# Converting float64 weights in three rounds, and two early steps instead of three, in a Fourier filter and MLP kernel

## The chip, the cores and the metric

The kernel runs on one core of a Trainium2 chip. The metric is device time in microseconds (us); lower is better. A core has TensorE (PE; its weight loads are listed as PEld), VectorE (DVE), ScalarE (ACT), GpSimd (POOL) and the sequencer SP, which here only issues transfers. Transfers issued by SP, ScalarE and GpSimd are carried by DMA engines.

## The reference

```python
X = np.fft.rfft(x, axis=1)              # x: 8 x 3008 x 256
y = np.fft.irfft(X * (filt_r + 1j * filt_i), n=3008, axis=1)
x = y.reshape(24064, 256)
h = x @ w_in                            # 256 -> 2048
g = h - np.tanh(h)
out = g @ w_out                         # 2048 -> 256
```

x and the filters arrive as float32. The two weight matrices arrive as float64 and are computed with as float32, so the kernel itself has to convert them.

## The kernel before

**Transform.** 3008 is 64 times 47. A batch is transformed with matmuls in three stages with a round trip through DRAM between them. `first` (line 291) multiplies two slices of x by a 64-point matrix (`pf`, L304), copies the result on ScalarE (L305) and has ScalarE store it to `ct1`. `middle` (line 348) loads `ct1` as `a2`, makes the 47-point products (`pz`), multiplies them by the filter (`uv`, `zs`), transforms back (`pe`) and stores to `ct2`. `last` (line 436) loads `ct2` as `e2` (`load_e2`, L417 and L425), makes the inverse 64-point product (`pu`, L447) and copies it to `ut` on ScalarE (L449).

**MLP.** For every group of `ut` and every quarter of the 2048 columns there is one step, numbered U. `up` makes seven products by `wu` instead of eight (banks X, Y, Z, L483); between them ScalarE copies X out as s1, u2 and u3 (L489). `shrink` approximates h − tanh(h) with ScalarE activations (L539, 540, 545) and VectorE products (L544, 548), and ends with `combine` (L462 to 465), four GpSimd operations that make the combinations for the seven products of `down` by `wd` (L590). `down(U − 2)`, `shrink(U − 1)` and `up(U)` run interleaved. The order is written out by hand: `up` calls back d, e (a piece of `down`), s (a piece of `shrink`) and t(0) to t(4).

**Units.** The eight batches are worked in the units (0), (1, 2), (3, 4), (5, 6), (7). While one unit's MLP runs, the `first` and `middle` of the next are put between its products by t(k): a list of positions says from which t(k) on the next piece is due. The first pieces are the `first` steps of the next unit. For unit 0 there are 24 such steps, of which EARLY have been done before the loop; the rest are spread over the positions from 0.24 on, `1.36 * 24 / (24 - EARLY)` apart.

**Prologue.** Unit 0's transform has nothing to run beside it. It is written separately, as one hand-ordered block (from L861): x in three chunks, `first0` (its copies and stores), then a loop over j = 0 to 15. Step j makes `pz` (L915) for two frequencies, finishes the step before (`back0`: `pe` L896 and L898, copy e L901, store to `ct2` L902), and makes uv and zs on VectorE (L922, L923). One set of filters, c, serves two steps. `filters_of(c)` (L803) fetches it with six GpSimd transfers (L814), after two memsets (L822) for the first three sets; `double_filters` (L839, L840) and `turned` (L848, L849) complete it on ScalarE, in the odd step before its first use. The loads of a2, of the matrices `fg` and of x go out on SP.

**Weights.** `converted` (L191) turns one tile of 128 x 512 float64 words into float32. It loads the words (L197). VectorE takes the mantissa's upper bits (L204), the exponent (L207) and the sign (L210); ScalarE scales the mantissa (L205) and the exponent (L209); VectorE adds the lower word (L211). After a `yield` VectorE clamps the exponent (L214), shifts and joins it with the sign (L215) and multiplies into `wu` or `wd` (L222). `weights` (L225) is a generator that orders such jobs, two to a quarter of the columns of one matrix, and has GpSimd make four combinations of a finished quarter (`sums`, L255 to L258). The ten jobs of five quarters are drawn in the prologue, one `next(ws)` to each step j (three raw tiles, four tiles for the rest, the latter shared with the x chunks). The six jobs of the last three quarters are drawn from t(0), t(2) and t(4) of the main loop (`late`). There a job's tiles are borrowed from the transform's pool, two of each tag: raw from `ft`, `it` from `uv`, `pt` from `zs`, `st` from `e1`, `ft` from `a2`.

**Filter copies.** In t(1) and t(3) of the main loop `copies` draws from `filters_d`, which clears parts of DRAM from a tile `zero` (also of tag `a2`; L955, L962, L964) and copies the filters to DRAM with SP's transfers (L814).

**Handover.** In step j = 14 of the prologue `first(1)` starts, which asks for x 0 and 1 (`load_x`, L283, three tiles), followed by rows 0 to 48 of e2 (L417). After the last `back0` come rows 48 to 64 of e2, then EARLY steps of `first(1)`, each of which first asks for the x two steps on; then `last(0)` and the main loop.

Of the kernel before, what the change touches and what calls it, by code (L numbers as in the profile page):

```python
# [14 lines left out]
AF = mybir.ActivationFunctionType  # L15
ALU = mybir.AluOpType
# [7 lines left out]
NK = NQ // 2  # L24
# [6 lines left out]
IM = 64  # L31
# [7 lines left out]
UNITS = [(0,), (1, 2), (3, 4), (5, 6), (7,)]  # L39
HALF = (NR + 1) // 2  # L40

EARLY = 3


def steps_of(unit):
# [97 lines left out]
def kernel(  # L143
# [24 lines left out]
    def dram(t, off, dims):  # L168
        return bass.AP(tensor=t, offset=off, ap=[list(d) for d in dims])
# [21 lines left out]
    def converted(tiles, src, dsts, queue):  # L191

        n = src.shape[-1] * (src.shape[1] if len(src.shape) == 3 else 1)
        t = tiles("raw", I64, n)
        queue.dma_start(t if len(src.shape) == 2 else  # L197
                        t.rearrange("p (h n) -> p h n", h=src.shape[1]), src)
        yield
        words = t.bitcast(I32).rearrange("p (n w) -> p n w", w=2)  # L200
        lo, hi = words[:, :, 0].bitcast(U32), words[:, :, 1]
        it, pt, st = (tiles(k, I32, n) for k in ("it", "pt", "st"))
        ft = tiles("ft", F32, n)
        V.tensor_scalar(out=it, in0=hi, scalar1=0xFFFFF, scalar2=None, op0=ALU.bitwise_and)  # L204
        ACT.activation(ft, it, AF.Identity, bias=1.0, scale=2.0 ** -20)  # L205

        V.tensor_scalar(out=pt, in0=hi, scalar1=20, scalar2=0x7FF,  # L207
                        op0=ALU.logical_shift_right, op1=ALU.bitwise_and)
        ACT.activation(pt, pt, AF.Relu, bias=exp_b)  # L209
        V.tensor_scalar(out=st, in0=hi, scalar1=-2 ** 31, scalar2=None, op0=ALU.bitwise_and)  # L210
        V.scalar_tensor_tensor(out=ft, in0=lo, scalar=2.0 ** -52, in1=ft,  # L211
                               op0=ALU.mult, op1=ALU.add)
        yield
        V.tensor_scalar_min(pt, pt, 255.0)  # L214
        V.scalar_tensor_tensor(out=pt, in0=pt, scalar=23, in1=st,  # L215
                               op0=ALU.logical_shift_left, op1=ALU.bitwise_or)
        pt = pt.bitcast(F32)
        for cols, dst, sign in dsts:
            f, p = ft[:, cols], pt[:, cols]
            if len(dst.shape) == 3:  # L220
                f, p = (v.rearrange("p (h n) -> p h n", h=dst.shape[1]) for v in (f, p))
            V.scalar_tensor_tensor(out=dst, in0=f, scalar=sign, in1=p, op0=ALU.mult, op1=ALU.mult)  # L222
        yield

    def weights(tiles, quarters, ahead):  # L225


        jobs = []
        for k in quarters:
            u = k % 4  # L230
            for h in range(2):
                if k < 4:
                    cols = slice(256 * u, 256 * u + 256)
                    src = bass.AP(tensor=moe_w_in.tensor, offset=128 * h * DFF + 256 * u,
                                  ap=[[DFF, 128], [DFF // 2, 2], [1, 256]])
                    dsts = [(slice(0, 256), wu[:, (0, 1)[h], cols], 1.0),
                            (slice(256, 512), wu[:, (6, 3)[h], cols], (1.0, -1.0)[h])]
                else:
                    t = 2 * u + h
                    cols = slice(128 * t, 128 * t + 128)  # L240
                    src = bass.AP(tensor=moe_w_out.tensor, offset=128 * t * DM,
                                  ap=[[DM, 128], [DFF // 2 * DM, 2], [1, DM]])
                    dsts = [(slice(0, 256), wd[:, 0:7:6, cols], 1.0),
                            (slice(256, 384), wd[:, 1, cols], 1.0),
                            (slice(384, 512), wd[:, 3, cols], -1.0)]
                jobs.append((src, dsts))

        def start(k):
            j = converted(tiles, *jobs[k], nc.sync)
            next(j)  # L250
            return j

        def sums(u):
            w = (wu if u < 4 else wd)[:, :, 256 * (u % 4):256 * (u % 4) + 256]
            G.tensor_sub(w[:, 4], w[:, 6], w[:, 3])  # L255
            G.tensor_sub(w[:, 5], w[:, 4], w[:, 0])
            G.tensor_sub(w[:, 2], w[:, 1], w[:, 5])
            G.tensor_sub(w[:, 6], w[:, 0], w[:, 6])  # L258

        began = [start(k) for k in range(ahead)]  # L260
        yield
        for k in range(len(jobs)):
            next(began[k])
            if k and k % 2 == 0:
                sums(quarters[k // 2 - 1])
            if k + ahead < len(jobs):
                began.append(start(k + ahead))
            yield
            next(began[k])
            yield  # L270
        sums(quarters[-1])
        yield
# [138 lines left out]
    def load_e2(p, c, t=None, rows=None):  # L411
        r, n = CHUNKS[p][c]
        if t is None:
            t = tr.tile([128, CH, DM], F32, tag="e2", bufs=2, name="e2")
        if rows is not None:
            for h, _, r_h, n_h in halves(p, r, n):
                nc.sync.dma_start(t[64 * h + rows.start:64 * h + rows.stop, 0:n_h, :],  # L417
                                  dram(ct2[p], (rows.start * RP + r_h) * DM,
                                       [[RP * DM, rows.stop - rows.start], [1, n_h * DM]]))
            return t  # L420
        if len(UNITS[p]) == 2:
            nc.sync.dma_start(t[:, 0:n, :], dram(ct2[p], r * DM, [[RP * DM, 128], [1, n * DM]]))
        else:
            for _, rows, r_h, n_h in halves(p, r, n):
                nc.sync.dma_start(t[rows, 0:n_h, :],  # L425
                                  dram(ct2[p], r_h * DM, [[RP * DM, 64], [1, n_h * DM]]))
        return t
# [6 lines left out]
    e2s, uts = {}, {}  # L434
# [321 lines left out]
    with tc.tile_pool(name="tr", bufs=2) as tr:  # L756
        with tc.tile_pool(name="pro", bufs=1) as pro, \
# [45 lines left out]
            def filters_of(c, to=None):  # L803


                n = 4 if c < NK // 4 - 1 else 3

                def put(row, m, v, i, n_s, src, off, dims):
                    if to is None:
                        dst = t[IM * v + row:IM * v + row + m, v, i:i + n_s, :]  # L810
                    else:
                        dst = dram(to, ((row * 2 + v) * NK + 4 * c + i) * DM,
                                   [[2 * NK * DM, m], [DM, n_s], [1, DM]])
                    (G if to is None else nc.sync).dma_start(dst, dram(src.tensor, off, dims))  # L814

                if to is None:
                    t = filt[c % 3]


                    if c < 3:  # L820
                        for v in range(2):
                            G.memset(t[IM * v + 32:IM * v + 64, v], 0.0)  # L822
                    if n == 3:
                        G.memset(t[IM:IM + 1, 1, 3], 0.0)
                for row, m in ((0, LO), (LO, 16), (LO + 16, HI - 16)):
                    sign = 1 if row < LO else -1
                    r0 = 4 * c + 1 + NQ * row if row < LO else NQ * (row - LO + 1) - 1 - 4 * c
                    for v, src in enumerate((filt_r, filt_i)):
                        put(row, m, v, 0, n, src, r0 * DM, [[NQ * DM, m], [sign * DM, n], [1, DM]])
                if n == 3:  # L830
                    for v, src in enumerate((filt_r, filt_i)):
                        put(v, LO - v, v, 3, 1, src, v * NQ * DM,
                            [[NQ * DM, LO - v], [DM, 1], [1, DM]])
                        put(LO, HI, v, 3, 1, src, NQ // 2 * DM,
                            [[NQ * DM, HI], [DM, 1], [1, DM]])
                return None if to is not None else t
# [24 lines left out]
            with tc.manual_schedule():  # L861
# [6 lines left out]
                pad = pro.tile([64, DM], F32, name="pad")  # L868
                G.memset(pad, 0.0)
                G.dma_start(dram(ct1[0], NR * 64 * DM, [[DM, 64], [1, DM]]), pad)  # L870
                fts = {0: filters_of(0)}
                gx = [pro.tile([IM + RP, 4, RP2], F32, name=f"gx{k}") for k in range(2)]
                for t in gx:
                    G.memset(t[32:64], 0.0)
# [30 lines left out]
                for j in range(NK // 2):  # L905
# [20 lines left out]
                    if j % 2 and c + 1 < NK // 4:  # L926
                        double_filters(fts[c + 1], c + 1)
                        turned(mats[c + 1][1], gx[(c + 1) % 2])
                    if j == NK // 2 - 2:
                        fs = first(1, z1)  # L930
                        next(fs)
                        e2s[0] = load_e2(*groups[0], None, slice(0, 48))
                back0()
                load_e2(*groups[0], e2s[0], slice(48, 64))
                for _ in range(EARLY):
                    next(fs)
                for _ in ws:
                    pass

# [155 lines left out]
```

## Time and profile before

| | |
|---|---|
| Time, median of 3 runs | 2882.22 us (2879.55 to 2883.24) |
| Profiled execution | 2881.08 us; span of the trace 2879.3 us; mean granted TensorE clock 0.984 |
| Busy: TensorE, VectorE, ScalarE, GpSimd | 2748.1, 1989.3, 1872.2, 1743.4 us |
| Moved by DMA | 217.46 MB, mean 76 GB/s |
| First `pz` of the prologue | 43.02 us |
| Last e copy of the prologue; last `ct2` store landed | 107.22; 109.98 us |
| First `pu` of the main loop | 117.08 us |

Every line below is from one execution under the profiler, and a time such as 117.08 is counted from the start of its span. The page's list of 40 slices gives each engine's busy share in tenths. A line of the timeline gives start, length, engine, line of the kernel and operation; a bracket gives the idle time just before it and what ended that. An engine's idle time costs something only where the engine that bounds the stage waits for it.

### The profile page before, as it was taken

How to read it: one execution, taken by the hardware profiler on the slowest of the kernel's cores; microseconds unless marked ns; L12 is line 12 of the kernel's file. 1: busy time of each engine (PE TensorE's matmuls, PEld its weight loads, DVE VectorE, ACT ScalarE, POOL GpSimd, SP SyncE). 2: the span in 40 equal slices, each digit the busy share in tenths (PEclk: the TensorE clock that was granted, in tenths of full speed). 3: DMA queues.
4: the chain of work that ended last, by engine and by line, in shares of the span. 5: the costliest groups of instructions: out<-in, count | busy, mean ns of one | idle time of the engine just before them, and what ended most of it. 6: DMA issues, size and time to landing. Idle time of an engine off the chain costs nothing.

```text
span 2879.3 us, 36469 instructions
## 1 busy us (share of the span) xinstructions
PE 2748.1 (95%) x12474; PEld 2278.9 (79%) x12474; DVE 1989.3 (69%) x2214; ACT 1872.2 (65%) x2460; POOL 1743.4 (61%) x1382
## 2 busy tenths in 40 slices
PE   5789999999999999999999999999999999999996
PEld 3467777888878787888877888888888888888885
DVE  4675666766776677766677777766777777777765
ACT  3555666666767676666666676666666676666663
POOL 4345777544677767645576777655476666555544
PEclk7889999999999999999999999999999999999998
DMA  9644443232233332222323233112233222110100
GB/s 270 180 150 116 114 110 91 62 93 81 70 76 84 76 75 53 57 81 83 87 71 75 68 78 81 36 45 67 51 75 81 53 55 56 24 28 16 26 11 16
DMA packets 328061, 217.46 MB, mean 76 GB/s; under 512 B 229085, under 2 KB 280405, under 8 KB 327674
## 3 DMA queue, kind: packets, MB, share of 16 engines
q1 hardware_dynamic: 273176, 160.50, 23.6%
q10 hardware_dynamic: 52738, 51.33, 5.9%
q0 software_dynamic: 1952, 3.22, 0.5%
q8 instruction: 100, 1.64, 0.2%
q14 instruction: 95, 0.78, 0.1%
HBM read 138.81 MB, written 79.17 MB: 76 GB/s over the span
## 4 chain that ended last, share of the span: by engine, by line
PE 69%; DVE 9%; ACT 8%; POOL 5%; issue 4%; DMA 3%; SPq 1%; ACTq 0%; DVEq 0%; POOLq 0%
PE o L590 27%; PE x L483 18%; PE z L483 8%; PE y L483 5%; PE pe L364 3%; PE pu L447 3%; DVE h L544 3%; PE pz L383 3%; ACT y L539 2%; PE pf L304 2%; ACT y L540 1%; POOL t L465 1%; ACT u L489 1%; DVE uv L398 1%; DVE h L519 1%
## 5 line engine op out<-in xcount | busy, mean ns | idle before, releaser
L590 PE MATMUL o<-t,wd 128*128 128x256 f32 (+2 forms) x3072 | 777.9, 376 | 1.8 <-POOL t L464 1.3
L544 DVE TENSOR_TENSOR h<-h,y 128x1024 f32<-128x1024 f32 (+2 forms) x384 | 589.7, 1536 | 256.1 <-ACT y L540 255.9
L462 POOL TENSOR_TENSOR t<-h 128x512 f32<-128x512 f32 (+2 forms) x192 | 240.1, 1250 | 767.5 <-DVE h L548 582.3
L590 PEld LDWEIGHTS o<-t,wd 128*128 128x128 f32 x3072 | 582.0, 191 | 74.4 <-POOL t L464 1.9
L483 PE MATMUL x<-tu,wu 128*128 128x256 f32 (+2 forms) x2304 | 592.2, 380 | 16.5 <-ACT u L489 15.5
L590 PE MATMUL o<-h,wd 128*128 128x256 f32 (+2 forms) x2304 | 581.6, 375 | 0.2 <-DVE h L548 0.2
L548 DVE SCALAR_TENSOR_TENSOR h<-sq,h 128x1024 f32<-128x1024 f32 (+2 forms) x384 | 566.6, 1476 | 20.8 <-ACT y L539 0.5
L483 PEld LDWEIGHTS x<-tu,wu 128*128 128x128 f32 x2304 | 430.2, 191 | 157.2 <-issue 73.2
L590 PEld LDWEIGHTS o<-h,wd 128*128 128x128 f32 x2304 | 431.3, 190 | 70.8 <-issue 18.5
L545 ACT ACTIVATE sq<-y,near_b 128x1024 f32<-128x1024 f32 (+2 forms) x384 | 435.4, 1134 | 5.8 <-DVE h L548 1.1
L539 ACT ACTIVATE y<-h 128x1024 f32<-128x1024 f32 (+2 forms) x384 | 400.0, 1042 | 14.8 <-ACT e L367 6.8
L489 ACT COPY s<-x 128x512 f32<-128x512 f32 (+2 forms) x192 | 110.7, 577 | 458.2 <-PE x L483 449.6
L540 ACT ACTIVATE y<-y 128x1024 f32<-128x1024 f32 (+2 forms) x384 | 399.3, 1040 | 12.2
L465 POOL TENSOR_TENSOR t<-t,h 128x512 f32<-128x512 f32 (+2 forms) x192 | 306.7, 1597 | 0.0
L489 ACT COPY u<-x 128x512 f32<-128x512 f32 (+2 forms) x384 | 219.2, 571 | 73.0 <-PE x L483 35.5
L399 POOL TENSOR_TENSOR zs<-zs,ft 128x512 f32<-128x512 f32 x112 | 166.3, 1485 | 142.3 <-ACT zs L397 142.2
L463 POOL TENSOR_TENSOR t<-h,t 128x512 f32<-128x512 f32 (+2 forms) x192 | 241.6, 1258 | 15.0
L464 POOL TENSOR_TENSOR t<-h 128x512 f32<-128x512 f32 (+2 forms) x192 | 249.5, 1300 | 0.0
L400 POOL TENSOR_TENSOR uv<-uv,zs 128x512 f32<-128x512 f32 x112 | 211.3, 1887 | 16.0 <-DVE uv L398 7.8
L483 PE MATMUL x<-ut,wu 128*128 128x256 f32 (+2 forms) x768 | 200.0, 383 | 12.2 <-DVE h L519 10.7
L483 PE MATMUL z<-tu,wu 128*128 128x256 f32 (+2 forms) x768 | 195.4, 377 | 0.5 <-DVE h L525 0.5
L483 PE MATMUL z<-ut,wu 128*128 128x256 f32 (+2 forms) x768 | 194.8, 376 | 0.0
(113 smaller groups left out, 3236.6 us busy)
## 6 DMA issues: line engine op xcount, KB each, us to landing
a<-ct SPq DMA_DIRECT2D x64, 384.0 KB
ct<-e ACTq DMA_DIRECT2D x128, 192.0 KB
ft<-filt SPq DMA_DIRECT2D x96, 256.0 KB
out_dram<-ot SPq DMA_DIRECT2D x1408, 16.0 KB
ct<-a ACTq DMA_DIRECT2D x80, 256.0 KB
x_sb<-in_x_dram SPq DMA_DIRECT2D x69, 256.0 KB
e<-ct SPq DMA_DIRECT2D x33, 512.0 KB
fg<-fg SPq DMA_DIRECT2D x40, 392.0 KB
```

Source lines behind the costliest of these rows:

```text
L462: G.tensor_sub(t[0], b[0][1], b[0][0])
L463: G.tensor_sub(t[1], b[1][1], t[0])
L464: G.tensor_sub(t[2], b[1][1], b[0][1])
L465: G.tensor_sub(t[3], t[1], b[1][0])
L483: nc.tensor.matmul(bank[:, k], wu[:, q - 1, (2 * u + k) * 128:(2 * u + k + 1) * 128], rhs[q - 1], start=(first and k == 0), stop=True, ski ...
L489: ACT.copy(t, X)
L539: ACT.activation(y[k], ht[k], AF.Arctan, scale=S)
L540: ACT.activation(y[k], y[k], AF.Square)
L544: V.tensor_mul(ht[k], ht[k], y[k])
L545: ACT.activation(sq[k], y[k], AF.Square, bias=near_b, scale=A)
L548: V.scalar_tensor_tensor(out=ht[k], in0=sq[k], scalar=K, in1=ht[k], op0=ALU.add, op1=ALU.mult)
L590: nc.tensor.matmul(product(q), wd[:, q - 1, (2 * u + k) * 128: (2 * u + k + 1) * 128], rhs[q - 1][:, k], start=(u == 0 and k == 0 and q == ...
```

## The change

- EARLY is 2 instead of 3.
- `converted` has three rounds with a `yield` between them: VectorE's three extractions; ScalarE's two activations; VectorE's mantissa, clamp, join and products.
- `weights` draws them in turn. In one draw a job gets its first round (and, from the fourth pass on, in every second pass, `sums` of a finished quarter is put after it). In the next draw the job gets its second round, the job before it the third, and then the load of the job two on is asked for. It takes two more draws than before in all.
- The memsets for filter sets 0, 1 and 2 leave `filters_of`. Those of sets 1 and 2 stand right after the transfers of set 0, so on GpSimd the transfers of sets 1 and 2 come before the first `sums`.
- `first(1)` starts in step j = 13 (its x 0 and 1 a step sooner); rows 0 to 48 of e2 are asked for in step 15.
- Rows 48 to 64 of e2 are asked for after the early steps of `first(1)`.

```diff
-EARLY = 3
+EARLY = 2
...
         V.tensor_scalar(out=it, in0=hi, scalar1=0xFFFFF, scalar2=None, op0=ALU.bitwise_and)
-        ACT.activation(ft, it, AF.Identity, bias=1.0, scale=2.0 ** -20)
-
         V.tensor_scalar(out=pt, in0=hi, scalar1=20, scalar2=0x7FF,
                         op0=ALU.logical_shift_right, op1=ALU.bitwise_and)
+        V.tensor_scalar(out=st, in0=hi, scalar1=-2 ** 31, scalar2=None, op0=ALU.bitwise_and)
+        yield
+
+        ACT.activation(ft, it, AF.Identity, bias=1.0, scale=2.0 ** -20)
         ACT.activation(pt, pt, AF.Relu, bias=exp_b)
-        V.tensor_scalar(out=st, in0=hi, scalar1=-2 ** 31, scalar2=None, op0=ALU.bitwise_and)
+        yield
         V.scalar_tensor_tensor(out=ft, in0=lo, scalar=2.0 ** -52, in1=ft,
                                op0=ALU.mult, op1=ALU.add)
-        yield
         V.tensor_scalar_min(pt, pt, 255.0)
...
-        for k in range(len(jobs)):
-            next(began[k])
-            if k and k % 2 == 0:
+        for k in range(len(jobs) + 1):
+            if k < len(jobs):
+                next(began[k])
+            if k > 2 and k % 2:
                 sums(quarters[k // 2 - 1])
+            yield
+            if k < len(jobs):
+                next(began[k])
+            if k > 0:
+                next(began[k - 1])
             if k + ahead < len(jobs):
                 began.append(start(k + ahead))
-            yield
-            next(began[k])
             yield
         sums(quarters[-1])
...
-
-
-                    if c < 3:
-                        for v in range(2):
-                            G.memset(t[IM * v + 32:IM * v + 64, v], 0.0)
...
+                for t in filt[0:1]:
+                    for v in range(2):
+                        G.memset(t[IM * v + 32:IM * v + 64, v], 0.0)
                 fts = {0: filters_of(0)}
+                for t in filt[1:]:
+                    for v in range(2):
+                        G.memset(t[IM * v + 32:IM * v + 64, v], 0.0)
...
-                    if j == NK // 2 - 2:
+                    if j == NK // 2 - 3:
                         fs = first(1, z1)
                         next(fs)
+                    if j == NK // 2 - 1:
                         e2s[0] = load_e2(*groups[0], None, slice(0, 48))
                 back0()
-                load_e2(*groups[0], e2s[0], slice(48, 64))
                 for _ in range(EARLY):
                     next(fs)
+                load_e2(*groups[0], e2s[0], slice(48, 64))
```

## The prediction, made before the changed kernel had run

> **What bounds the kernel now.** I read the page's engine shares and its 40 slices first, to learn where TensorE (PE) is not busy.
>
> ```profile
> PE 2748.1 (95%) x12474; PEld 2278.9 (79%) x12474; DVE 1989.3 (69%) x2214; ACT 1872.2 (65%) x2460; POOL 1743.4 (61%) x1382
> ...
> PE   5789999999999999999999999999999999999996
> ...
> PEclk7889999999999999999999999999999999999998
> DMA  9644443232233332222323233112233222110100
> ```
>
> PE is busy 2748.1 of 2879.3 us; from the fourth slice on (a slice is 72 us) it is full. Of its 131 idle us about 64 lie before 216 us, and the change works only there: the prologue (unit 0 alone, to 107 us), the handover (107 to 123) and the first six steps of the main loop, U0 to U5 (to 216). From then on every engine's instructions are the same in the same order, and PE bounds them: a shift won by 216 us is kept to the end, one for one.
>
> Next the table of windows of 5 us (busy time and count of PE, PEld, DVE, ACT, POOL; clock, DMA share, GB/s):
>
> ```profile
> 50.00:55.00 5.00, 4.59 (x22) 3.32 (x21) 4.04 (x8) 3.96 (x7) 4.44 (x8) 1.00 1.03 234
> 55.00:60.00 5.00, 3.60 (x16) 2.44 (x15) 4.93 (x8) 1.01 (x2) 3.24 (x6) 1.00 1.07 250
> 60.00:65.00 5.00, 1.20 (x5) 0.58 (x3) 0.96 (x3) 2.97 (x4) 1.45 (x3) 0.73 1.07 278
> ...
> 110.00:115.00 5.00, 0.64 (x1) 0.50 (x2) 0.00 (x0) 0.00 (x0) 0.00 (x0) 0.85 0.93 281
> 115.00:120.00 5.00, 3.65 (x11) 1.95 (x10) 0.00 (x0) 1.17 (x2) 0.14 (x1) 0.50 0.49 149
> ```
>
> The DMA engines are full (about 250 GB/s) here, and at 60 to 65 us every engine waits for them. At 110 to 115 us nothing computes while one x tile travels. Then the timeline (start, length, line, count; in brackets what was waited for) shows SP's order at the handover and all waits of PE over 1 us from there to 216:
>
> ```profile
> 98.23 12.66 SPq L417 DMA_DIRECT2D e<-ct  x4
> 110.93 1.37 SPq L283 DMA_DIRECT2D x_sb<-in_x_dram  x3
> ...
> 114.36 2.04 PE L304 MATMUL pf<-x_sb,wf_sb 128*128 128x512 f32 x2 [6.05 <-DMA x_sb<-in_x_dram]
> 117.08 2.08 PE L447 MATMUL pu<-s_sb,e 128*128 128x128 f32 x8 [0.68 <-ACT a L305]
> ...
> 142.20 2.08 PE L483 MATMUL x<-tu,wu 128*128 128x256 f32 x4 [3.61 <-ACT u L489]
> 146.87 2.07 PE L483 MATMUL x<-tu,wu 128*128 128x256 f32 x4 [2.60 <-ACT u L489]
> 162.73 1.13 PE L483 MATMUL x<-tu,wu 128*128 128x256 f32 x4 [1.58 <-ACT u L489]
> 186.30 2.08 PE L483 MATMUL x<-tu,wu 128*128 128x256 f32 x4 [3.77 <-ACT u L489]
> 201.38 1.16 PE L304 MATMUL pf<-x_sb,wf_sb 128*128 128x512 f32 x2 [4.23 <-DMA x_sb<-in_x_dram]
> ```
>
> The third early step (pf, L304) waits for an x tile that SP issues behind the last e rows, and pu, the main loop's first work, stands behind it. The u copies wait on ScalarE behind its conversions. One conversion:
>
> ```profile
> 83.16 0.63 ACT L205 ACTIVATE conv<-conv 128x512 f32<-128x512 int32 x1 [0.40 <-DVE conv L210]
> 83.70 0.71 ACT L209 ACTIVATE conv<-conv,exp_b 128x512 int32<-128x512 int32 x1
> 84.31 0.56 ACT L901 COPY e<-pe 96x512 f32<-96x512 f32 x1
> ...
> 83.83 0.69 DVE L211 SCALAR_TENSOR_TENSOR conv<-raw,conv 128x512 f32<-128x512 uint32 x1 [0.72 <-ACT conv L205]
> ```
>
> VectorE stands 0.72 us for ScalarE; ScalarE had stood 0.40 for VectorE.
>
> [...] 243 to 278 GB/s whatever queue adds to it. So a transfer moved earlier takes from what travels there. [...] 0.50 at 115 to 120 us, and the first four of pu's matmuls run at twice their later cost. [...] three L222 products took 3.92 us at 192.27, beside GpSimd's combine, against 0.83 at 164.71.
>
> **Part 1: the prologue.** (a) *Three rounds.* Four conversions of the loop have VectorE waits of 0.88, 0.67, 0.72 and 0.73 (its timeline): 3.0 us go. The two ScalarE activations (1.15 us from 83.16 to 84.31) move from the even step to the odd one, ahead of the filter copies L839/840 (1.04 each) that uv of the next pair waits for. ScalarE of a pair then runs e, store, conversion, two copies, two gx. In the old trace the same work took 6.2 us (82.18 to 88.40). Now the chain from e over conversion 1.15, copies 2.1, zs 0.65, pe 0.9 to the next e, with e and its store 1.0 and hand-offs of 0.4 to 0.5 each, gives 6.7 to 7.35. The starts of uv in even steps were 45.16, 51.78, 63.66, 73.51, 80.82, 87.49, 95.87, 101.93: steps of 6.6, 11.9, 9.9, 7.3, 6.7, 8.4, 6.1. So the undisturbed pairs lose up to 1, while the disturbed ones (11.9, 9.9, 8.4) can come down. Seven pairs of 7.35 end at 96.6.
>
> (b) *Filters.* The memsets of filters 1 and 2 (1.94 us a pair) now stand ahead of gx, and both filters' GpSimd transfers ahead of the first sums, which waited 23.1 us for VectorE. 12 issues of about 0.55 us each move from 36.8–45.2 to about 12–20 us: 0.75 MB. In return a raw buffer is free only after round three, so raw load 4 (0.5 MB) slides from 29 to behind 38 us: net 0.24 MB less in the full stretch, 1.0 us at 250 GB/s. The memsets cost nothing: GpSimd idled there. Against it, ScalarE's fourth ct1 store waits for raw 0 (to 21.17, by its timeline), and the filters now travel beside that: up to +1.5. From 42 us the loop moves some 13.1 MB, 52.4 us at 250: uv of step 14 not before 94.5. (c) *Order on SP.* A raw load may now stand at SP's head until round three ends; a2 and slot loads are behind it, but they are issued a whole pair ahead. Conversion data arrive some 10 us before use instead of 19 to 25: enough beside a 7-us pair. Value: uv of step 14 at about 99 instead of 101.93, **−2.5**, carried to the last e copy; bounds −5.5 (the DMA floor) and +3 (ScalarE's order plus the crowded start).
>
> **Part 2: the handover.** x 0 and 1 are asked for one j-step earlier, behind a2 only; x 2 and 3 now stand ahead of e rows 48:64, which wait for the last ct2 store (109.98) anyway. So pf no longer waits 6.05. After the last e rows (issued 110.47, plus the 2.2 to 3 us such a load takes) pu can start at 113.3 to 113.5 instead of 117.08: **−3.6** (−3.1 to −4.0). The colder clock is no new loss: pu ran at 0.50 before. The third step moves into the loop: 0.86 us of PE, which is inside Part 3 (17 in the loop by the end of U5 instead of 16; 19 with the early ones, in both).
>
> **Part 3: U0 to U5**, walked by the order of instructions on each queue. U0 +0.25, U1 +0.3: ScalarE's conversion stands behind s, not ahead of u, so 3.61 and 2.60 shrink to about half, but the second conversion lands behind u3. U2 +1 to +2.6: ScalarE's second conversion needs the a2-tagged tile, of which there are two, and the filters' zero tile holds one; so it stands until round three of the first ends (about 157), s and y behind it. U3: the 3.77 wait goes (the conversion's three VectorE operations are done a step before), but the x tile for this step stands on SP behind a raw load that waits for round three, to about 181.5: net 0. U4: one pf step fewer stands ahead of X, so the 4.23 wait, for an x tile just issued, moves behind other work: X of U5 at about 210.8 instead of 214.35. U5: the last sums now stand behind combine (5.3 us) on GpSimd, 0 to +0.9. VectorE's crowding beside GpSimd comes out equal (two 3.9-us rounds each way). Sum from X to X: **−2.4**, bounds −6.5 and +2.5.
>
> **Sum.** −2.5 −3.6 −2.4 = −8.5: span 2870.8. The profiled execution took 2881.08, the median is 2882.22 (2879.55 to 2883.24), so the forecast is 2873.7. 0.2% (5.8 us) is about what a measurement here can tell from no change.
>
> **Rivals.** (A) *The prologue's gain is hidden:* conversions ahead of the filter copies hold seven pairs at the old total, and U0–U5 only trade waits. For: 6.7 to 7.35 is no shorter than the quiet pairs. Against: the stall at 60 to 65 is 5 us, and VectorE's 3.0 go. The handover alone: 2878.6. (B) *SP becomes the bound, slower:* raw loads of the main loop wait for round three at SP's head, x loads behind them. By my walk x lands 4.2, 3.6 and 8.2 us late for three pf steps: 16.0, in place of the 5.8 of waits at 162.73, 186.30 and U1's 0.46. +10.2 −3.6 = +6.6: 2888.8. It decides from where the raw tile is freed later than the x tile is needed, if the prologue gives nothing. For: one queue, in order. Against: rounds two and three are one j-step or quarter of U apart, and VectorE had been done within a step in the old trace. (C) *All waits go:* DMA floor −5.5, handover −3.6, and of the 11.6 us of u waits (3.61, 2.60, 1.58, 3.77) five more than I count: −14.1, 2868.1. For: no wait within a round. Against: the two a2 tiles and combine.
>
> **Chances.** Forecast 0.43, A 0.22, B 0.13, C 0.22. Faster by over 0.2%: 0.36 of the first, all of C, 0.03 of A: 0.61. Slower: most of B, 0.01 of A: 0.11. Same: 0.28. From 2866 to 2886 leaves out most of B and a third of C.
>
> **What would show it.** Right: no VectorE wait at the mantissa (L213); uv of step 14 at 97 to 101; pu within 114; no pf between the last e copy and pu; no 4-us wait for x near 200. Wrong: pairs over 7.5 us with ScalarE never idle (A); pf waiting for x over 3 us at 155 to 182 with SP on a raw load (B); a stall as at 60 to 65 that stays; a shift at 216 us that PE doesn't keep.

## The result, and the profile after

The changed kernel takes 2897.03 us in the median of 6 runs (2890.11 to 2903.09), the kernel before 2881.26 us beside it; the ratio is 1.0055, 95% interval 1.0039 to 1.0070. It is slower by 15.8 us where 8.5 less were forecast, and lies outside the range 2866 to 2886.

The page of the changed kernel, the lines that answer to those of before:

```profile
PE 2757.1 (95%) x12474; PEld 2281.8 (79%) x12474; DVE 1985.2 (69%) x2214; ACT 1873.1 (65%) x2460; POOL 1745.1 (60%) x1382
...
PE   5878999999999999999999999999999999999996
...
PEclk7889999999999999999999999999999999999998
DMA  8644444223323332132232223112223222110100
```

The instructions are as many as before; PE is busy 9 us longer, with more of its work at a lower granted clock (mean 0.980 for 0.984), and stands 139 us instead of 131. The digits of the first slices (5878 for 5789, DMA 8644 for 9644) say where: at the start, and with DMA engines less full. Windows of 5 us of the changed kernel (busy time and count of PE, PEld, DVE, ACT, POOL; clock, DMA share, GB/s):

```profile
40.00:45.00 5.00, 0.00 (x0) 0.00 (x0) 0.00 (x0) 3.70 (x5) 2.58 (x4) 0.50 0.42 96
...
50.00:55.00 5.00, 5.00 (x13) 3.28 (x12) 4.69 (x10) 0.00 (x0) 1.22 (x3) 0.50 0.74 174
55.00:60.00 5.00, 4.37 (x19) 3.15 (x18) 2.04 (x5) 4.16 (x6) 2.06 (x4) 0.96 0.90 220
60.00:65.00 5.00, 3.08 (x14) 2.07 (x14) 4.93 (x11) 1.27 (x3) 2.25 (x5) 1.00 0.84 231
65.00:70.00 5.00, 2.85 (x12) 1.96 (x11) 1.10 (x3) 4.21 (x6) 3.89 (x6) 0.91 0.96 233
...
120.00:125.00 5.00, 2.05 (x8) 1.78 (x8) 0.00 (x0) 0.28 (x1) 0.24 (x1) 0.53 0.89 238
```

The dead window at 60 to 65 us, which was forecast to go, is only in part gone: PE was busy 1.20 us in it, and the worst window here, 5 us later as the whole loop is, has 2.85 for PE, but 1.10 for VectorE (0.96 before). And the loop's first product had started at 43 us, while here PE and VectorE do nothing from 40 to 45 us; the DMA engines, full from 50 to 65 us in the old loop (1.03 to 1.07), are at 0.74 to 0.90; and the handover's wait, at 110 to 115 us before, now lies at 120 to 125. The time by stretches, between the same instructions of both traces:

| Stretch (us) | before | after | difference | forecast |
|---|---|---|---|---|
| start to first pz | 43.02 | 48.14 | +5.1 | |
| first pz to last e copy | 64.20 | 68.12 | +3.9 | with the line above −2.5 |
| last e copy to pu | 9.86 | 6.38 | −3.5 | −3.6 |
| pu to X of U5 | 97.27 | 108.27 | +11.0 | −2.4 |
| X of U5 to X of U7 | 32.18 | 33.30 | +1.1 | 0 |
| X of U7 to the end | 2632.77 | 2631.79 | −1.0 | 0 |

The main loop is where most went. Its timeline (start, length, line, count; in brackets the wait) around PE's waits:

```profile
144.15 0.80 SPq L288 DMA_DIRECT2D x_sb<-in_x_dram  x2
160.57 0.38 SPq L197 DMA_DIRECT2D raw<-in_moe_w_out_dram  x1
161.04 1.97 SPq L963 DMA_DIRECT2D ct<-zero  x4
163.12 1.02 SPq L288 DMA_DIRECT2D x_sb<-in_x_dram  x2
...
188.60 0.40 SPq L197 DMA_DIRECT2D raw<-in_moe_w_out_dram  x1
189.10 0.40 SPq L288 DMA_DIRECT2D x_sb<-in_x_dram  x1
...
159.86 0.69 DVE L213 SCALAR_TENSOR_TENSOR ft<-raw,ft 128x512 f32<-128x512 uint32 x1
...
149.04 1.10 PE L309 MATMUL pf<-x_sb,wf_sb 128*128 128x512 f32 x2 [2.85 <-DMA x_sb<-in_x_dram]
...
167.25 2.04 PE L309 MATMUL pf<-x_sb,wf_sb 128*128 128x512 f32 x2 [6.39 <-DMA x_sb<-in_x_dram]
...
193.07 2.05 PE L309 MATMUL pf<-x_sb,wf_sb 128*128 128x512 f32 x2 [4.27 <-DMA x_sb<-in_x_dram]
...
216.80 2.08 PE L488 MATMUL z<-tu,wu 128*128 128x256 f32 x4 [3.39 <-DVE h L530]
```

PE stood 6.39 us at 167.25 for an x tile, which SP asked for only at 163.12, behind four stores of zeros and a raw load issued at 160.57. That load overwrites the words that the mantissa operation L213 of an earlier job, at 159.86, was the last to read; SP had issued nothing since 144.95, 15.6 us. The view of waits sums this for SP, from 124 to 232 us (waiting line and what it waited for; us in all, times, longest):

```profile
SPq L197 <- DVE ft L213: 22.3, 2, 15.5
SPq L197 <- DVE pt L215: 20.4, 2, 11.5
```

In the old main loop SP also stood with a raw load at its head (its view of waits, 118 to 226 us):

```profile
SPq L197 <- DVE ft L211: 30.7, 4, 12.6
```

But there the wait ended in the draw that asked for the load, since the last read of the words (L211) stands in a job's first round. The one long x wait of the old loop (4.23 us at 201.38) has no raw load ahead of it: the last had left SP at 159.13.

In the prologue, one pair of steps, by the timeline:

```profile
72.60 0.68 DVE L213 SCALAR_TENSOR_TENSOR conv<-raw,conv 128x512 f32<-128x512 uint32 x1
...
87.66 0.69 DVE L929 TENSOR_TENSOR uv<-pz,filt 128x512 f32<-128x512 f32 x1 [3.63 <-ACT filt L839]
...
73.31 0.55 SPq L197 DMA_DIRECT2D raw<-in_moe_w_in_dram  x1
73.96 0.69 SPq L340 DMA_DIRECT2D a<-ct  x1
...
82.71 2.04 PE L922 MATMUL pz<-a,fg 94*128 94x256 f32 x4 [1.53 <-DMA a<-ct]
...
84.34 0.58 ACT L908 COPY e<-pe 96x512 f32<-96x512 f32 x1 [4.14 <-DMA ct<-e]
...
85.32 0.63 ACT L210 ACTIVATE conv<-conv 128x512 f32<-128x512 int32 x1 [0.40 <-ACT e L908]
...
86.58 1.04 ACT L839 COPY filt<-filt 64x1024 f32<-64x1024 f32 x1
```

In the loop the change does what it says: the mantissa L213 has no wait in its bracket. But the raw load leaves SP only after it, at 73.31; a2 leaves behind the raw load and lands for pz at 82.71; e waits 4.14 us for the stores of older e tiles to land; and the conversion stands between e and the filter copy that uv waits 3.63 us for. VectorE waits for no conversion there any more, and yet the pairs (from uv of one even step to the next) take 8.5, 9.9, 8.9, 10.0, 7.8, 8.3 and 6.9 us. The views of waits over the loop, before (40 to 110 us) and changed (45 to 118), show where the time went: the waits for e's stores are as long as they were, those of uv for the filter copies have more than doubled.

```profile
ACT e L901 <- DMA ct<-e: 11.4, 5, 5.5
DVE uv L922 <- ACT filt L839: 6.7, 3, 3.7
...
DVE uv L929 <- ACT filt L839: 15.9, 7, 3.6
ACT e L908 <- DMA ct<-e: 11.2, 3, 4.1
```

### The profile page after: what moved, and what is told of

Read it like the earlier page. It is cut to its first block, busy times and chain, and to the rows that moved or that the text cites. A ratio compares the mean times of both kernels' runs of the same rounds, so it can differ in the third digit from the quotient of the medians.

```text
span 2896.0 us, 36480 instructions
## 1 busy us (share of the span) xinstructions
PE 2757.1 (95%) x12474; PEld 2281.8 (79%) x12474; DVE 1985.2 (69%) x2214; ACT 1873.1 (65%) x2460; POOL 1745.1 (60%) x1382
## 4 chain that ended last, share of the span: by engine, by line
PE 69%; ACT 9%; DVE 9%; POOL 5%; issue 4%; DMA 3%; ACTq 1%; SPq 0%; DVEq 0%; POOLq 0%
PE o L595 27%; PE x L488 18%; PE z L488 8%; PE y L488 5%; PE pe L369 3%; PE pu L452 3%; DVE h L549 3%; PE pz L388 3%; ACT y L544 2%; PE pf L309 2%; ACT y L545 1%; POOL t L470 1%; ACT u L494 1%; DVE h L553 1%; DVE uv L403 1%
## 5 line engine op out<-in xcount | busy, mean ns | idle before, releaser
L488 PE MATMUL y<-ut,wu 128*128 128x256 f32 (+2 forms) x768 | 194.5, 376 | 0.0
```

Of the source, the lines that this page charges most:

```text
L488: nc.tensor.matmul(bank[:, k], wu[:, q - 1, (2 * u + k) * 128:(2 * u + k + 1) * 128], rhs[q - 1], start=(first and k == 0), stop=True, ski ...
```

## The experiments

All twelve were also timed beside the kernel before, whose median there was about 2880.4 us. The ratio is not the quotient of the two medians, and can differ from it by some 2 us. The measures of each profiled run, in us:

| Kernel | first pz | to last e copy | to pu | pu to X of U7 | median | ratio (95%) |
|---|---|---|---|---|---|---|
| before | 43.0 | 64.2 | 9.9 | 129.5 | | 1 |
| changed | 48.1 | 68.1 | 6.4 | 141.6 | 2897.0 | 1.0055 (1.0039–1.0070) |
| e1 handover alone | 43.4 | 62.9 | 6.9 | 128.2 | 2877.6 | 0.9983 (0.9972–0.9994) |
| e2 late in two rounds | 47.6 | 65.2 | 6.9 | 128.2 | 2887.5 | 1.0022 (1.0015–1.0030) |
| e3 filters late | 42.7 | 67.9 | 6.3 | 136.5 | 2896.2 | 1.0053 (1.0033–1.0072) |
| e4 four raw tiles | 48.1 | 68.2 | 6.7 | 129.0 | 2889.5 | 1.0028 (1.0014–1.0042) |
| e5 e2 and e3 | 43.4 | 67.2 | 6.6 | 128.7 | 2882.3 | 1.0005 (0.9993–1.0017) |
| e6, e10 raw later | 43.6, 43.0 | 65.4, 64.4 | 6.2, 6.2 | 131.3, 128.5 | 2879.9, 2878.5 | 0.9992 (0.9983–1.0001), 0.9990 (0.9983–0.9997) |
| e7, e11 copies first | 44.4, 42.9 | 67.4, 64.6 | 6.5, 6.9 | 127.9, 131.7 | 2880.6, 2882.0 | 0.9995 (0.9984–1.0007), 1.0002 (0.9993–1.0010) |
| e8, e12 both | 43.3, 44.1 | 62.3, 62.0 | 6.7, 6.7 | 127.1, 125.5 | 2875.9, 2876.7 | 0.9983 (0.9972–0.9994), 0.9986 (0.9979–0.9992) |
| e9 filters early alone | 48.2 | 59.4 | 9.9 | 124.3 | 2881.9 | 1.0002 (0.9993–1.0010) |

A cell of one trace can be 3 us off its mean: pu to X of U7 differs by 6 us among kernels with the same instructions there (125.5 to 131.7 with the new handover and late conversions in two rounds; 136.5 and 141.6 in e3 and the changed kernel, which share the changed main loop), the loop by 3 (65.2 to 68.2 with the changed kernel's order).

### e1: the handover alone

```diff
 # before.py
-EARLY = 3
+EARLY = 2
...
-                    if j == NK // 2 - 2:
+                    if j == NK // 2 - 3:
                         fs = first(1, z1)
                         next(fs)
+                    if j == NK // 2 - 1:
                         e2s[0] = load_e2(*groups[0], None, slice(0, 48))
                 back0()
-                load_e2(*groups[0], e2s[0], slice(48, 64))
                 for _ in range(EARLY):
                     next(fs)
+                load_e2(*groups[0], e2s[0], slice(48, 64))
```

> The kernel before with the handover's edits alone: EARLY 2, first(1) a step sooner, rows 0:48 of e2 in step 15, rows 48:64 after the early steps; conversions and filters as before. Theory (the handover works, the loss lies in conversions and filters): last e copy at 107 as before, pu 3.3 to 3.8 us sooner than 117.1, that is at about 113.5, and no x wait over 3 us before 200 but those of before; total -3 to -5 us. Rival (moving the third step into the main loop costs there, with x loads late): pu as sooner, but X of U5 no sooner than 214, total within 1 us of before.

Pu started at 113.17, where both theories had it, and waits for nothing but the last rows of e2:

```profile
105.72 1.88 PE L304 MATMUL pf<-x_sb,wf_sb 128*128 128x512 f32 x4
...
113.17 2.04 PE L447 MATMUL pu<-s_sb,e 128*128 128x128 f32 x8 [5.57 <-DMA e<-ct]
```

X of U5 came at 208.83 instead of 214.35, so the third step costs nothing in the main loop. This part of the change is sound: 2.8 us faster by the medians, 4.9 by the ratio.

### e2: the late conversions in two rounds

`converted` and `weights` of the changed kernel take a flag that restores the old code and order; only the late call uses it.

```diff
 # after.py
-            late, copies = weights(tiles1, range(5, 8), 2), filters_d()
+            late, copies = weights(tiles1, range(5, 8), 2, False), filters_d()
```

> The changed kernel with the six late conversions (quarters 5 to 7) back in two rounds in the old order; the prologue's in three. Theory (the 11 us lost between pu and U5 come from round three in the main loop): pu stays at about 122.6, and from pu to X of U7 it takes 129 to 130 us, as before, instead of 141.6; total some 11 us below the changed kernel's 2897, about 2886. Rival (they come from the two early steps, the third moved into the loop): from pu to X of U7 still over 138, total over 2894.

Pu to X of U7 took 128.2 us, 13.4 less than in the changed kernel, and the median fell by 9.5 us. The two early steps are not the cause, round three in the main loop is. Pu itself came 3 us sooner than in the changed kernel, which was not expected: the loop of that run was shorter, within the spread named above.

### e3: filters 1 and 2 behind the first sums

```diff
 # after.py
-                fts[1] = filters_of(1)
...
-                            fts[c + 2] = filters_of(c + 2)
+                            if c:
+                                fts[c + 2] = filters_of(c + 2)
...
                     next(ws, None)
+                    if j == 0:
+                        fts.update({k: filters_of(k) for k in (1, 2)})
```

> The changed kernel with filters 1 and 2 fetched after the first sums, in step 0 of the loop. Theory (their 0.75 MB, moved to 12 to 24 us, delay the x chunks and raw 0, and with these the ct1 stores): the last ct1 store of first0 is issued near 34 instead of 41, first pz at 43 to 44 instead of 48.1; later steps as in the changed kernel, total -4 to -5 us. Rival (the conversions' order on ScalarE and VectorE delays the stores): first pz stays at 47 to 48, total no lower than 2895.

The last ct1 store left at 33.93 instead of 39.95 and the first pz started at 42.73 instead of 48.14; so the filters' transfers, not the conversions' order, made the start late. What held ScalarE in the changed kernel is seen on its timeline there:

```profile
18.76 5.91 ACTq L803 DMA_DIRECT2D ct<-a  x2
24.71 1.07 ACT L799 COPY a<-pf 128x512 f32<-128x512 f32 x2 [9.49 <-DMA raw<-in_moe_w_in_dram]
```

The second of two ct1 stores was out at 24.7 us, and the profile puts the wait down to raw 0, whose first reader on VectorE starts at 24.09. In the kernel before these are 21.8 and 21.17, in e3 21.8 and 21.27, in e9 24.8 and 24.20: the two stores are out about 0.6 us after that reader starts, each time. Why they wait for that load no run shows. By its first reader raw 0 is 2.9 us late (24.09 for 21.17), and at the later stores the delay grows to the 6.1 us of the last one (39.95, against 33.85 in the kernel before). The median of e3 (4 runs, 2892 to 2900) doesn't show the gain; e5 against e2, which differ by this edit alone, does: 2882.3 against 2887.5.

### e4: four places for the late raw words

```diff
 # after.py, above and in tiles1
+            raws = []
...
+                if k == "raw":
+                    if not raws:
+                        big_raw = tr.tile([128, 2, n], dtype, tag="ft", bufs=2, name=k)
+                        raws[:] = [big_raw[:, h] for h in range(2)]
+                    return raws.pop(0)
```

> The changed kernel with four places for the late raw words (two in each of the two buffers of tag ft) in place of two, so that a raw load never waits for round three of the job just begun. Theory (SP's head: raw load waits, x loads behind it): the three waits of pf for x in U1 to U3 (2.85, 6.39, 4.27 us) fall under 1 us each, together some 11 us less, from pu to X of U7 about 131 to 133 instead of 141.6, total about 2887. Rival (the order of conversions on ScalarE and VectorE and the GpSimd sums hold PE): pf waits shift to waits for u and h, from pu to X of U7 still over 138.

All three rounds stay, and so does their order; only the raw load has somewhere to go. The waits of PE over 1 us behind the one of pu, to 222 us, are these:

```profile
138.20 1.65 PE L488 MATMUL x<-tu,wu 128*128 128x256 f32 x4 [2.35 <-ACT u L494]
...
152.81 2.08 PE L488 MATMUL x<-tu,wu 128*128 128x256 f32 x4 [4.93 <-ACT u L494]
...
168.21 1.13 PE L488 MATMUL z<-tu,wu 128*128 128x256 f32 x4 [2.01 <-DVE h L530]
...
206.12 1.37 PE L488 MATMUL z<-tu,wu 128*128 128x256 f32 x4 [3.40 <-DVE h L530]
```

No pf waits for x over 0.5 us. Pu to X of U7 fell from 141.6 to 129.0, 12.6 of the 13.4 us of e2 (against e3's 136.5, the same main loop once more, it is 7.5), and the median by 7.5 of its 9.5; SP's waits on the mantissa fell to one, 8.3 us. The rival was half right in kind, not in size: a u wait grew from 1.78 to 4.93.

### e5: e2 and e3 together

> The changed kernel with filters 1 and 2 after the first sums and the late conversions in two rounds: of the change only the prologue's three rounds and the handover stay. If the losses at the start (5.4) and in the main loop (13.4) are separate and add up: first pz near 43, last e copy near 110.6, pu near 117, pu to X of U7 128.2, X of U7 at 245, 1 us before the kernel before; total about 2880. If they are not separate, X of U7 differs from 245 by more than 2 us.

X of U7 came at 245.9, and the two losses add. What is left of the change, three rounds in the prologue and the handover, costs 1.9 us by the medians, which can't be told from nothing (0.9993 to 1.0017), but is 4.8 more than the handover alone (e1); the loop took 67.2 us against 62.9 there. So in this order the prologue's rounds lose what the handover gains.

### e6, e7, e8: SP's order and ScalarE's order, each alone and both

```diff
 # e5's kernel; e6: in weights
             if k < len(jobs):
                 next(began[k])
+            if k and k - 1 + ahead < len(jobs):
+                began.append(start(k - 1 + ahead))
...
-            if k + ahead < len(jobs):
-                began.append(start(k + ahead))
...
 # e7: in the loop over j
-                    next(ws, None)
-                    if j == 0:
-                        fts.update({k: filters_of(k) for k in (1, 2)})
                     if j % 2 and c + 1 < NK // 4:
                         double_filters(fts[c + 1], c + 1)
                         turned(mats[c + 1][1], gx[(c + 1) % 2])
+                    next(ws, None)
+                    if j == 0:
+                        fts.update({k: filters_of(k) for k in (1, 2)})
```

> As e5, with each raw load of the prologue asked for one draw later, in the even step behind a2 and fg instead of ahead of them. Theory SP (three rounds put a raw load, which waits for round three, ahead of a2 and fg in SP's queue, and so bunch a pair's transfers): no pz waits for a2 over 0.5 us, pairs of 6.5 to 7.5, last e copy 3 to 4 us sooner than in e5, near 107. Rival ScalarE (the conversion ahead of the filter copies makes the pair longer): pairs stay at 7.5 to 9.5, last e copy within 1 us of e5. Rival DMA (the stores of e and the filters land late because the engines are full): some pairs stay near 9 with ScalarE waiting for stores.

> As e5, with the draw of an odd step put after the filter copies and gx, so that ScalarE's conversion follows them. Theory ScalarE: each pair 1.1 us shorter, last e copy some 5 us sooner than in e5, near 105 to 106. Theory SP: pairs as in e5, since a2 and the raw load go out no sooner; last e copy within 1.5 us of e5.

> e6 and e7 together. If both theories hold a part: pairs near 6.5, last e copy at 103 to 105, pu at 110 to 112, total about 2873 to 2876, below the kernel before and e1. If only one holds: as the better of e6 and e7. If the DMA engines set the pairs: last e copy not before 106, as in e1.

From first pz to last e copy they took 65.4, 67.4 and 62.3 us, against 67.2 in e5; the last e copy came at 109.0 (near 107 by the theory of SP), 111.8 (105 to 106 by that of ScalarE, as late as in e5 by that of SP) and 105.6 (103 to 105). The first two differences are within what one trace is worth, so each of the three ran once more:

> The kernel of e6 once more, since one trace of the prologue is worth 1 to 3 us at most (the same prologue took from first pz to last e copy 68.1, 68.2 and 65.2 us in three kernels). If SP's order alone helps: first pz to last e copy again near 65.4 (e6), against 67.2 and 67.9 of e5 and e3, and a median below e5's. If not: near 67.

> The kernel of e7 once more, for the same reason. If ScalarE's order alone does nothing: first pz to last e copy again near 67.4 (e7). If it helps: under 65.5.

> The kernel of e8 once more, with more rounds. First pz to last e copy 61.5 to 63.5 again (62.3 in e8, 64.2 in the kernel before, 62.9 in e1), X of U7 at 239 to 242, total 3 to 6 us below before.

They gave 64.4, 64.6 and 62.0. With five loops in the changed kernel's order at 65.2 to 68.2 (mean 67.3), the raw load behind a2 is worth about 2.4 us, the copies ahead of the conversion about 1.3 (67.4 and 64.6, so not settled), and both 5.2. With both, three rounds are about as quick as two rounds were (62.1 against 63.6 of before and e1): e still waits for its stores, and the filter copy and uv wait behind e. In e8 (the view of waits from 40 to 112 us, then its timeline):

```profile
ACT e L922 <- DMA ct<-e: 12.2, 5, 5.2
...
60.46 0.58 ACT L922 COPY e<-pe 96x512 f32<-96x512 f32 x1 [5.19 <-DMA ct<-e]
61.52 1.04 ACT L854 COPY filt<-filt 64x1024 f32<-64x1024 f32 x1 [0.47 <-ACT e L922]
62.65 0.69 DVE L944 TENSOR_TENSOR uv<-pz,filt 128x512 f32<-128x512 f32 x1 [4.22 <-POOL wu L263]
```

The uv waits for a filter copy, 15.9 us in the changed kernel, are 8.4 in e8: 4.2 that the view lists so, and the 4.22 above, which it puts down to GpSimd although the filter copy ends last (62.56). The DMA engines, at 0.52 to 1.06 in the changed kernel's windows of 5 us from 50 to 95 us, are at 0.92 to 1.07 in e8 (0.80 to 1.07 before). This suggests that in the order of e8 full engines hold the loop again, and that what VectorE no longer waits for buys nothing there. E8's expectation had named this for a last e copy not before 106 (105.6 here, 106.1 in e12); e8's order with fewer bytes in the loop was not tried. E8 and e12 are below the kernel before, like e1; two rounds with the new handover and three rounds so ordered cannot be told apart.

### e9: the early filters alone

```diff
 # before.py
+                fts.update({k: filters_of(k) for k in (1, 2)})
                 mats = {0: load_slots(0, pro)}
...
-                fts[1] = filters_of(1)
...
-                            fts[c + 2] = filters_of(c + 2)
+                            if c:
+                                fts[c + 2] = filters_of(c + 2)
```

> The kernel before with one part of the change alone: the memsets and transfers of filters 1 and 2 at the start, ahead of the first sums; conversions, EARLY and the order on SP as before. Theory (the early transfers delay x, raw 0 and the ct1 stores by themselves): first pz at 47 to 48.5 instead of 43, and part of it given back in the loop, where 0.75 MB fewer are moved: last e copy 2 to 5 us later than 107, total +2 to +5. Rival (it is the conversions' new order that makes the start late, the filters only together with it): first pz within 1.5 us of 43, total within 2 us of before.

```profile
48.21 3.75 PE L916 MATMUL pz<-a,fg 94*128 94x256 f32 x8 [9.08 <-DMA a<-ct]
107.65 0.58 ACT L901 COPY e<-pe 96x512 f32<-96x512 f32 x1 [1.86 <-DMA ct<-e]
```

The first pz is 5.2 us late by the filters alone. But the old loop gives nearly all of it back: 59.4 us instead of 64.2, and its last e copy is 0.4 us later, where 2 to 5 were expected. Its DMA engines were full (0.97 to 1.03 from 45 to 80 us in this run), and with 0.75 MB fewer to move it was 4.8 us shorter: the old loop was bound by them. At 250 GB/s (the rate of the kernel before from 55 to 60 us) these bytes are 3.0 us, by estimate; the rest is not explained. The changed loop was bound by its order, and did not use the relief: with filters early it took 68.1, 65.2 and 68.2 us, with filters late 67.9 and 67.2.

## Why the prediction was wrong, step by step

**What bounds the kernel: right in the main.** All was decided before about 250 us. The difference at X is +17.7 us at U8, +18.9 at the fourth step from the end, and +16.7 in the span. "One for one" holds less well in single traces: e1 is 5.1 us ahead at X of U7 and 1.0 at the end. The last section tells where the lead went.

**Part 1(a), three rounds: right in kind, wrong in what bounds a pair.** The 3.0 us of VectorE waits went. The pair was put at 6.7 to 7.35 by ScalarE's chain; it took 6.9 to 10.0, since the waits for e's stores (11.2 us in all) and for a2 were not in that chain.

**Part 1(b), filters: the term was mis-sized.** Up to +1.5 was allowed for the crowded start; it was +5.1 (e3: 5.4; e9: 5.2), because ScalarE's ct1 stores go out behind raw 0 and everything after stands behind them. The filters' issues were put at about 12 to 20 us; they went out from 12.60 to 25.9, with waits of 2.11, 1.77 and 0.98 us for transfers of their own. The relief in the loop was counted as 1.0, net of the raw load moved the other way. It is real, 4.8 in e9, only not in this loop.

**Part 1(c), order on SP: the step that failed in the prologue's loop.** It said that a2 and slot loads behind a raw load are issued a whole pair ahead, and that this is enough. It wasn't: a2 left SP only when the raw load ahead of it could, and a pair's raw, a2 and slot loads then went out within 2 us of each other (73.31 to 74.74); pz waited for a2 (1.53 us at 82.71). Undoing that alone (e6, e10) took 2.4 us off the loop, together with ScalarE's order (e8, e12) 5.2.

**Part 2, handover: right.** −3.5 for −3.6, and −3.0 in e1. The granted clock at pu was as low as before: 0.50 from 115 to 120 us then, 0.53 from 120 to 125 here. (From 110 to 115 us before, three x tiles were under way, not one: SP's line at 110.93 has x3. The wait is the same.)

**Part 3, U0 to U5: failed most, by 13 us.** The forecast knew that a raw load waits for round three, and wrote a late x down for U3, with "net 0"; but it took rounds two and three of a job for one draw apart. In the main loop a raw tile has two places, so the load asked for in job k's second draw takes job k's own tile, which is free after its third round, two draws later. For that time SP issued nothing (15.6 us up to 160.57). E4 shows it: places alone, without a change of order, take 12.6 of the 13.4 us away. Measured, X to X was 2.9, −1.2, 8.1, 0.1 and 1.2 us longer in U0 to U4, 11.0 in all; in e3, with the same main loop, 0.3, −2.2, 8.3, −1.1 and 0.9, 6.3 in all. So the term that went wrong is U2, with +1 to +2.6 forecast: SP's hold of 15.6 us ends there, and it has the longest x wait, 6.39 and 6.55 us in the two traces. The 2.9 us of U0 are no wait for x: e4 keeps them (15.0 us for U0, 14.5 in the changed kernel), and e3 does not have them (11.8; before 11.6). U4 was to gain and did not: instead of the 4.23 us for x it waits 3.39 us for h (3.40 in e3 and e4, in e2, with two rounds, there is none over 1 us). That wait belongs to the three rounds, not to the raw tiles; its cause was not followed further.

**The rivals.** B had the mechanism and its place, at 0.13: x late by 4.2, 3.6 and 8.2 for three steps; the trace has waits of 2.85, 6.39 and 4.27. Its argument against, that rounds are a draw apart, was the same error. It fell short (2888.8) since it let the prologue lose nothing. A's mechanism, conversions ahead of filter copies, is worth 2.8 us once SP's order is mended (5.2 less 2.4); alone it is not settled. C fell: in the loop e waits 11 to 12 us for its stores, before, changed and in e8.

**Shared DMA engines.** That a transfer moved earlier takes from what travels there is borne out by e9 in both directions, 5.2 us lost and 4.8 gained. In the kernel before, the queues were at work on the 16 DMA engines side by side (view of DMA by window): from 60 to 65 us SP's, GpSimd's and ScalarE's took 66.0, 28.5 and 12.8% of the engines' time, 107% in all, at 278 GB/s; from 45 to 50 us the first two took 73.9 and 32.1%, at 243 GB/s. No run moved a transfer to another queue. In the changed kernel a chain hung on the transfers delayed at the start (the last ct1 store went out at 39.95 instead of 33.85), while its loop did not become shorter by the relief. The forecast's 250 GB/s holds for the loop alone: its own lines begin at 234, not 243, and from 20 to 30 us engines as full (1.06 and 1.07) moved 403 and 394 GB/s in the kernel before.

## What to carry to other kernels

Before moving the last read of a buffer later, look at which load takes that buffer next, on which queue it is issued, and what stands behind it: the load can be asked for in the same place and still block its queue until that read is done (SP issued nothing for 15.6 us here). VectorE no longer waited for ScalarE's conversions (3.0 us in the old loop), and that gained nothing here, since the freed slots were not on the chain that bounds the loop: stores, loads and filter copies. Bytes moved out of the loop (0.75 MB) came with 4.8 us less where the transfers bound it (e9), and with nothing where its order did (67.2 and 67.9 us with filters late, 65.2 to 68.2 early).

## What the runs showed of the hardware

After waits of the same length, the same work of PE took 1.7 us longer in one run than in another, at a lower granted clock. After a wait of 2.59 us in the kernel before and of 2.58 in e1, near 505 us, eight matmuls of PE ran as follows (timeline; same instructions):

```profile
509.03 1.89 PE L590 MATMUL o<-t,wd 128*128 128x256 f32 x8
```

```profile
504.00 3.31 PE L590 MATMUL o<-t,wd 128*128 128x256 f32 x8
```

The four matmuls ahead of them took 0.92 and 1.23 us. The granted clock was 1.00 in the kernel before (508 to 512 us) and 0.57 in e1 (503 to 507). In five of the fourteen traces these eight took 1.89 us, in nine (the changed kernel's among them) 3.06 to 3.43, after waits of 2.57 to 2.60 us in all. It is not the kernel that decides: e7 and e11 are one kernel and fell on different sides, and so did e8 (1.89 us) and e12 (3.39). What decides, no run shows.

Near the end, the eight matmuls behind a stage of small ones (128 x 48) differ by 1.4 us, with no wait over 0.2 us listed in the 7 us ahead of them. The granted clock was 1.00 there in the kernel before (2790 to 2794 us); for e1 it was not measured. Before and in e1:

```profile
2790.75 1.96 PE L590 MATMUL o<-h,wd 128*128 128x256 f32 x8
```

```profile
2787.51 3.38 PE L590 MATMUL o<-h,wd 128*128 128x256 f32 x8
```

From the fourth-last X to the last it took 46.2 us before, 44.5 in the changed kernel, 49.5 in e1. So e1, 5.1 us ahead at X of U7, loses 1.7 by the fourth-last X and 3.3 up to the last, gains 0.8 behind it, and shows 1.0 in its span. Single runs of these kernels spread by 6 to 18 us.
